# Three of eight w_out remainders on ScalarE and GpSimd in place of VectorE, and a new written order

## The chip, the cores and the metric

The kernel runs on one core of one Trainium2 chip. The core has five engines, each with a queue of its own that it works through in order: TensorE (PE in the profile; PEld is its loading of weights), VectorE (DVE), ScalarE (ACT), GpSimd (POOL) and SyncE (SP, which only issues transfers). Engines wait for one another through semaphores. The metric is the device time of one execution in microseconds (us).

## The reference

The reference is a Nystrom attention followed by a multiplicative feed-forward layer, with 8 batches, 8 heads, 576 positions, head size 64 and 32 landmarks:

```python
q_lm, k_lm = means of q and k over 18 neighbouring positions
A, Bm, C = softmax(q k_lm'), softmax(q_lm k_lm'), softmax(q_lm k')
Z = Bm' / (norms);  six times: Z = 2 Z - Z Bm Z
x = (A Z C v) as (4608, 512)
a, b = x @ w1, x @ w2
h = a * b @ w3
out = h @ w_out
```

All inputs and outputs are f32. The part that the change touches is small: the product of w3 (1024x1024) and w_out (1024x512). The kernel forms `w3 @ w_out` once, so that the last two lines become one product with a 1024x512 matrix, `w34`.

## The kernel before

**Two numbers for one.** TensorE works on f16 here. To keep the precision of w3 and w_out, the kernel splits each, scaled by `WSC` = 16, into a high part (the f16 nearest to it) and a remainder (the f16 nearest to what is left), and adds three products: high times high, high times remainder, remainder times high. For each of the eight slices c of w_out (128x512), ScalarE writes the high part (`woh{c}`, line 329) and VectorE the remainder (`wol{c}`, line 334), in one instruction that scales, subtracts and rounds:

```python
nc.vector.scalar_tensor_tensor(out=wo[:, 1, c, :], in0=wof[c // 2][:, c % 2, :], scalar=WSC,
                               in1=wo[:, 0, c, :], op0=ALU.mult, op1=ALU.subtract)
```

The f32 slices stand two by two in four buffers `wof`, which lie in space that later holds `u` and `ab`; the profile therefore names them `u` and `ab`.

**w3, a block row at a time.** For each of eight block rows j, four transfers bring 128x1024 of w3 (`w3n{j}`, three buffers), VectorE transposes it in two halves (`tr{j}0`, `tr{j}1`, line 340), ScalarE makes the high parts (`wh`, line 347) and VectorE the remainders (`wl`, line 355). TensorE then does eight steps `mm{j}0` to `mm{j}7` of three matmuls; for j = 0 they are split into `mh0{c}`-like first products (`mh{c}`, which need no remainder) and the other two (`mm0{c}`). `wo{j}` (line 388) stores the result.

**The attention, in sixteen quads** n (half a batch each). GpSimd's queue issues the K and Q loads (`lq{n}0`, `lq{n}1`, line 449) and the loads of w1 and w2 (`lw`, line 467). VectorE transposes (`T`, line 474). The landmark means come from TensorE for quads 0 and 1 (`mp`) and from GpSimd for all others (`ma`, `mb`, lines 482 and 489); ScalarE copies them (`mk`, lines 508 and 510) and VectorE turns them (`lt`). TensorE makes the scores (`S`, `A`). For `S`: VectorE's maximum `sm` (line 540), TensorE's `sw`, VectorE's `sb`, ScalarE's exponentials `se`, VectorE's `ct`. For `A`: VectorE's `ar` (line 583) and `am` (line 589), GpSimd's `as` (line 595), ScalarE's `ae`, VectorE's sums `au` (lines 609 and 610), GpSimd's `an` (line 623), VectorE's `aT` (line 632).

**The batches.** The batches stand in five groups of 1, 2, 2, 2 and 1. For each group TensorE and VectorE take turns in the iteration for Z (`N`, `no`, then `x{i}_0`, `y{i}_0` up to 4, `Z`, `zo`); then come `C`, `W` and `U` for each batch, the dense products `d` with `e` on ScalarE and `f` on VectorE, and the outputs `g`, `h` and `st`.

**The order.** Nothing orders itself at run time. `ORDER` (line 39) names all 1339 tasks one after another; each engine's queue is this list with the other engines' tasks left out. Numbers behind a colon choose buffers and PSUM banks. In the table of tasks, `deps` say who waits for whom.

**Gates.** Four small copies on GpSimd (`gw0` to `gw3`, line 394) each read one element of a w_out buffer, so that GpSimd's queue waits there until that buffer has landed. All K and Q loads from quad 2 on, and the loads of w1 and w2, stand behind the fourth. So w_out and the first of w3 do not share the transfer engines with them.

Of the kernel before, what the change touches and what calls it, by code (L numbers as in the profile page):

```python
# [11 lines left out]
ALU = mybir.AluOpType  # L12
# [27 lines left out]
w3n0a.0 w3n0.0:0 zz w3n0a w3n0 lq00:0 ca wu0:0 cc wf0a.0 wf0s.0 lq01 tab wf0s cb wf1s.0 lq10:1 wf1s lq11 wf2s.0  # L40
wf0a wf2s wf1a.0 wu1:1 wf1a wf2a.0 wu2:2 wf2a wu3:3 T00:0 cd tr00:4.0 wf3s.0 wh00 wl00 tr01:5 woh0 gw0 wf3s ce
mp0:6 woh1 wol0 wh01 mh0:7 wol1 mm00 mk0:0 wf3a.0 T01 mm01 wl01 lt0 T10:1 woh2 gw1 wf3a S0:0.1 A0:2.3 woh3 sm0:0
mh1 mh2 ar0:0 w3n1.0:1 mh3 sw0 mp1:4 wol2 w3n1.1 am0:1 w3n1.2 woh4 gw2 w3n1 wol3 w3n2.0:2 woh5 mh4 wol4 mm02
w3n2.1 mm03 wol5 w3n2.2 mh5 woh7 gw3 w3n2 mm04 T11 as0 mm05 w3n3.0:0 woh6 wol7 w3n3.1 mk1:1 mh6 lq20:2 wol6
w3n3.2 lq21 sb0 mm06 tr10:6.1 w3n3 se00:0 lq30:3 mh7 lt1 mm07 wh10 tr11:5 lq31 S1:2.3 ae0 wl10 lw00 w3n4.0:1
A1:4.0 wo0 w3n4.1 au0 lq40:0 mm10:6 wh11 w3n4.2 lq41 mm11 w3n4 ar1:1 bo0:0 an0:0 mm12 tr20:7.0 mm13 lq50:1 am1:2
wh20 se01 wl11 as1 tr21:0 mm14 wl20 lw10 wh21 w3n5.0:2 mm15 w3n5.1 aT0:0 ae1 ma2:0 mm20:4 wl21 w3n5.2 mm16 w3n5
sm1:3 mm17 au1 mm21 mb2 ct0:0 mm22 bo1 mm23 T20:0 mm24 tr30:1.1 sw1 T21 wh30 N0:5.4 mm25 tr31:7 an1:1 mk2:0 mm26
sb1 bt0 w3n6.0:0 wl30 w3n6.1 mm27 no0:0 lw11 wo1 w3n6.2 mm30:0 se10:1 lq51 wh31 lt2 mm31 ma3:0 T30:1 A2:1.6 wl31
x0_0:2 w3n6 tr40:5.0 mm32 y0_0:1 wh40 mm33 ar2:0 lq60:2 se11 mm34 mb3 wl40 wo2 S2:7.2 am2:5 mm40:1 T31 mm41  # L50
tr41:6 mm35 sm2:6 w3n7.0:1 x0_1:3 as2 mk3:1 lv0.0:0 aT1:1 mm36 y0_1:2 ct1:1 sw2 lq61 x0_2:5 wh41 lt3 ae2 T40:0
lq70:3 A3:4.3 w3n7.1 lq71 wl41 mm37 ma4:0 ar3:1 mm42 wo3 mm43 y0_2:0 am3:7 w3n7.2 mm44 sb2 tr50:6.1 se20:0 mm45
as3 au2 wh50 x0_3:3 mm46 w3n7 mb4 y0_3:1 ae3 tr51:4 mm47 wl50 wh51 au3 wo4 mm50:0 se21 mm51 lv0.1 bo2:1 T41
S3:5.7 an2:0 ct2:2 mk4:0 mm52 T50:1 x0_4:3 lq80:0 bo3 mm53 lt4 lv0.2 wl51 ma5:0 S4:6.1 aT2:2 mm54 sm4:8 A4:2.4
sm3:9 sw4 lv0 mm55 mb5 y0_4:2 sb4 T51 mm56 se40:1 tr60:3.0 mm57 se41 ar4:0 sw3 wh60 Z0:6 lv1.0:1 wo5 wl60 sb3
tr61:1 lq81 mm60:2 mk5:1 lv1.1 T60:0 an3:1 mm61 wh61 ct4:3 mm62 ma6:0 se30:0 lt5 mm63 lv1.2 wl61 se31 lv1 A5:4.0
T61 lv2.0:2 mm64 tr70:3.1 lv2.1 S5:5.1 am4:1 lw01 wh70 lv2.2 mm65 lq90:1 sm5:2 mm66 as4 wl70 mm67 lv2 aT3:3 sw5
mb6 tr71:7 mm70:3 ae4 lv3.0:3 sb5 ar5:1 mm71 lv3.1 se50:1 lv3.2 wh71 mm72 T70:1 lv3 C0:5.0 am5:4 wl71 as5 mk6:0
au4 lq91 se51 mm73 lv4.0:0 zo0:0 wo6 ma7:0 co0:0.5 lv4.1 ae5 ct3:0 lv4.2 W0:4 mm74 lt6 wp0:0 wq0 au5 S6:7.1 lv4
an4:0 U000:6.2.0.1 mm75 sm6:7 bo5 mb7 bo4 lv5.0:1 uo0001 A6:0.5 T71 uo0000 sw6 N1:4.0 sb6 T80:0 se60:0 lv5.1  # L60
U011:2.6 ar6:0 se61 uo0110 lv5.2 U001:7.1 bt1 am6:3 uo0111 an5:1 U010:0.5 lv5 uo0011 ct5:1 mm76 mk7:1 as6 T81
mm77 no1:0 C1:2.6 uo0010 ma8:0 ae6 uo0101 lt7 au6 wo7 uo0100 S7:1.7 lv6.0:2 co1:1.5 A7:4.5 mb8 lv6.1 sm7:1
d000:3.0 lv6.2 lv6 d010:2.6 ar7:1 e000:0 lv7.0:3 sw7 aT4:4 lv7.1 e010:1 x1_0:3 sb7 am7:4 lv7.2 se70:1 d002:4.5
lv7 y1_0:1 an6:0 se71 d011:2.1 f000:0 e002:2 d001:3.7 T90:1 e011:0 as7 mk8:0 d030:0.4 f002:1 f010 d022:2.5
lq100:2 f011 e030:2 x1_1:6 lq101 f030 e022:1 e001:0 C2:0.1 lt8 lq110:3 T91 bo6:0 ae7 ma9:0 y1_1:2 f001 f022
ct6:0 x1_2:2 lv8.0:0 A8:4.3 lv8.1 co2:0.0 lq111 lv8.2 d032:6.7 lq120:0 ar8:0 lv8 d020:5.0 mb9 e032:2 lv9.0:1
d031:1.3 f032 lv9.1 e020:0 y1_2:0 lv9.2 d012:4.6 f020 d021:7.5 am8:6 e012:1 g00:2 f012 e021:2 aT5:5 as8 mk9:1
au7 x1_3:0 S8:4.6 lq121 ae8 g01 lt9 f021 ma10:0 e031:0 y1_3:1 g30:7 h0:0 f031 sm8:9 g31 aT6:0 sw8 T100:0 h3:1
x1_4:5 mb10 S9:1.0 st3.0 sb8 T101 se80:0 A9:2.3 lv9 bo7 y1_4:2 g10:7 se81 st3 sm9:5 Z1:4 ct8:2 g11 zo1:1 an7:1
# [94 lines left out]
def kernel(  # L164
# [83 lines left out]
    def dve(cols):  # L248
        return 0.07 + cols / 960.0
# [142 lines left out]
    def gate(c):  # L392
        def fn():
            nc.gpsimd.tensor_copy(out=gates[:, c:c + 1], in_=wof[c][:, 1, 0:1])
        return fn
# [671 lines left out]
```

## Time and profile before

| | |
|---|---|
| median of 3 runs | 269.22 us (268.96 to 269.9) |
| the profiled execution | 268.93 us |
| its span, first to last instruction | 267.2 us |
| TensorE busy | 254.8 us |
| VectorE busy | 191.2 us |
| ScalarE busy | 161.5 us |
| GpSimd busy | 136.9 us |
| granted TensorE clock | 0.996 |
| transfers | 37.33 MB, mean 140 GB/s |

The last matmul ends at 262.4 us; the rest of the span is the last output's copy and its transfer. In rows of a view, "x8" is a count of instructions, "out<-in" names the tiles, and a bracket at the end of a timeline row gives the idle time of the engine before it and who ended it. A row of the chain gives start, length and what was at work. Neighbouring instructions on VectorE overlap by some 0.08 us in these rows, so that one of 0.68 us takes 0.60 us of its queue.

### The profile page before, as it was taken

How to read it: one execution, taken by the hardware profiler on the slowest of the kernel's cores; microseconds unless marked ns; L12 is line 12 of the kernel's file. 1: busy time of each engine (PE TensorE's matmuls, PEld its weight loads, DVE VectorE, ACT ScalarE, POOL GpSimd, SP SyncE). 2: the span in 40 equal slices, each digit the busy share in tenths (PEclk: the TensorE clock that was granted, in tenths of full speed). 3: DMA queues.
4: the chain of work that ended last, by engine and by line, in shares of the span. 5: the costliest groups of instructions: out<-in, count | busy, mean ns of one | idle time of the engine just before them, and what ended most of it. 6: DMA issues, size and time to landing. Idle time of an engine off the chain costs nothing.

```text
span 267.2 us, 9564 instructions
## 1 busy us (share of the span) xinstructions
PE 254.8 (95%) x3948; PEld 167.4 (63%) x3948; DVE 191.2 (72%) x458; ACT 161.5 (60%) x415; POOL 136.9 (51%) x159
## 2 busy tenths in 40 slices
PE   8688999999999999999999999999999999999992
PEld 3343444344568955689868457877866699467662
DVE  1799999999999999999999787643672267203340
ACT  2555364745597467988757899634115975564452
POOL 4548999999999999999787511000110000000000
PEclk9999999999999999999999999999999999999998
DMA  7999999999966896289903333232713020415355
GB/s 173 277 233 213 234 238 231 240 261 234 200 156 178 146 245 140 51 179 250 160 9 82 81 83 81 66 81 60 206 55 83 4 61 2 92 28 139 80 119 139
DMA packets 22668, 37.33 MB, mean 140 GB/s; under 512 B 3552, under 2 KB 7904, under 8 KB 22624
## 3 DMA queue, kind: packets, MB, share of 16 engines
q1 hardware_dynamic: 16240, 24.33, 36.4%
q0 software_dynamic: 5696, 11.54, 24.3%
q10 hardware_dynamic: 688, 0.85, 1.0%
q8 instruction: 31, 0.51, 0.9%
q14 instruction: 13, 0.11, 0.1%
HBM read 38.80 MB, written 9.44 MB: 181 GB/s over the span
## 4 chain that ended last, share of the span: by engine, by line
PE 67%; POOL 14%; DVE 7%; ACT 5%; issue 3%; DMA 2%; DVEq 0%; POOLq 0%; ACTq 0%
PE bank L245 67%; POOL ls L489 5%; POOL ls L482 4%; DMA nat<-in_k_dram 2%; ACT lm L510 2%; POOL ea L595 2%; DVE bank L340 1%; DVE wo L334 1%; POOL nat L449 1%; ACT u L833 1%; DVE tiny L609 1%; DVE T L474 1%; POOL w L467 1%; ACT ec L559 1%; DVE tiny L589 1%
## 5 line engine op out<-in xcount | busy, mean ns | idle before, releaser
L914 DVE TENSOR_TENSOR ab<-asb,bank 128x384 f16<-128x384 f16 x96 | 49.4, 543 | 36.6 <-ACT asb L908 33.7
L245 PE MATMUL bank<-aT,u 128*128 128x192 f16 x768 | 69.4, 246 | 0.0
L245 PE MATMUL bank<-w,ab 128*128 128x512 f16 (+1 forms) x296 | 69.1, 374 | 0.0
L245 PEld LDWEIGHTS <-u 128*128 128x128 f16 x768 | 63.6, 98 | 6.0 <-issue 0.6
L908 ACT CAST asb<-bank 128x384 f16<-128x384 f32 x96 | 43.9, 487 | 27.4 <-PE bank L245 21.6
L245 PE MATMUL bank<-wo,w3t 128*128 128x512 f16 x192 | 46.3, 380 | 2.7 <-DVE wo L334 2.1
L245 PEld LDWEIGHTS <-ab 128*128 128x128 f16 x296 | 27.5, 98 | 26.3 <-issue 2.2
L489 POOL TENSOR_TENSOR ls<-ls 128x128 f32<-128x128 f32 (+2 forms) x56 | 40.8, 729 | 3.8
L928 ACT ACTIVATE osb<-bank 128x512 f32<-128x512 f32 x35 | 21.0, 605 | 28.3 <-PE bank L245 26.3
L623 POOL TENSOR_TENSOR ah<-ea,tiny 128x576 f16<-128x576 f32 x16 | 18.6, 1162 | 35.2 <-DVE tiny L711 26.7
L833 ACT CAST u<-bank 128x512 f16<-128x512 f32 x64 | 34.0, 616 | 3.0 <-PE bank L245 3.0
L482 POOL TENSOR_TENSOR ls<-nat 128x1152 f32<-128x1152 f16 x14 | 33.4, 2384 | 1.3 <-ACT asb L908 0.7
L245 PEld LDWEIGHTS <-w3t 128*128 128x128 f16 x192 | 17.3, 98 | 24.5 <-issue 5.1
L474 DVE STREAM_TRANSPOSE T<-nat 128x576 f32<-128x576 f32 x32 | 24.0, 750 | 5.6 <-DMA nat<-in_k_dram 5.6
L595 POOL TENSOR_TENSOR ea<-ea,tiny 128x608 f32<-128x608 f32 x16 | 19.8, 1241 | 9.6 <-DVE tiny L589 6.0
L559 ACT ACTIVATE ec<-bank,tiny 128x288 f32<-128x288 f32 x32 | 16.0, 502 | 7.1 <-DVE tiny L551 7.0
L245 PE MATMUL bank<-T 32*32 32x288 f16 (+1 forms) x320 | 18.5, 291 | 1.6 <-DVE T L516 1.6
L245 PE MATMUL bank<-vb,ecT 64*64 64x128 f32 x576 | 18.7, 272 | 0.0
L245 PEld LDWEIGHTS bank<-vb,ecT 64*64 64x64 f32 x576 | 16.7, 133 | 1.9 <-ACT u L833 0.4
L347 ACT ACTIVATE w3t<-bank 128x512 f16<-128x512 f32 x16 | 9.5, 593 | 12.3 <-DVE bank L340 12.1
L245 PE MATMUL bank<-w,wT 64*32 64x512 f16 x512 | 16.8, 378 | 0.0
L245 PE MATMUL bank<-xz 32*32 32x64 f32 (+1 forms) x768 | 16.5, 214 | 0.2 <-DVE xz L768 0.2
(78 smaller groups left out, 299.9 us busy)
## 6 DMA issues: line engine op xcount, KB each, us to landing
vb<-in_v_dram SPq DMA_DIRECT2D x64, 144.0 KB, 4.6
out_dram<-osb SPq DMA_DIRECT2D x70, 128.0 KB, 2.8
nat<-in_k_dram POOLq DMA_DIRECT2D x16, 288.0 KB, 8.6
nat<-in_q_dram POOLq DMA_DIRECT2D x16, 288.0 KB, 7.4
w3n<-in_moe_w_dram SPq DMA_DIRECT2D x30, 128.0 KB, 8.3
w<-in_moe_w_dram POOLq DMA_DIRECT2D x4, 512.0 KB, 12.4
ab<-in_moe_w_out_dram SPq DMA_DIRECT2D x8, 128.0 KB, 6.0
u<-in_moe_w_out_dram SPq DMA_DIRECT2D x4, 128.0 KB, 6.5
```

Source lines behind the costliest of these rows:

```text
L245: nc.tensor.matmul(out_, lhsT, rhs, start=start, stop=stop, **({} if pos is None else {"tile_position": pos}))
L347: nc.scalar.activation(out=w3t[at(f"w3t{j}")][:, 0, 4 * h:4 * h + 4].rearrange("p e g i -> p (e g i)"), in_=bank(at(f"w3f{j}{h}")), func=A ...
L474: nc.vector.transpose(out=Ts[at(f"T{n}")][:, GRP * t:GRP * t + GRP] .rearrange("p r l e -> p (r l e)").bitcast(FP32), in_=nats[at(f"nat{n} ...
L482: nc.gpsimd.tensor_tensor(out=l, in0=nat[:, :, 0:9, :], in1=nat[:, :, 9:18, :], op=ALU.add)
L489: nc.gpsimd.tensor_tensor(out=l[:, :, x:x + m, :], in0=l[:, :, x:x + m, :], in1=l[:, :, y:y + m, :], op=ALU.add)
L559: nc.scalar.activation(out=ecs[at(f"ec{n}")][:, hp, :], in_=two(f"pS{n}")[hp][:, 0:288], func=AXF.Exp, scale=SCALE, bias=t[:, 2 + hp:3 + h ...
L595: nc.gpsimd.tensor_tensor(out=ea, in0=ea, in1=tinies[at(f"ta{n}")][:, 0:19].unsqueeze(2).to_broadcast([128, 19, M]), op=ALU.subtract)
L623: nc.gpsimd.tensor_tensor(out=ahs[at(f"ah{n}")].rearrange("p g m r -> p g r m"), in0=eas[at(f"ea{n}")][:, 0:GRP, :].rearrange("p (g r) m - ...
L833: nc.scalar.copy(out=uu[at(f"u{b}{qd}")][:, wi, 512 * half:512 * half + 512], in_=bank(at(f"pU{b}{wi}{half}{qd}")))
L908: nc.scalar.copy(out=asb[at(f"as{b}{j}{ch}")], in_=d1_ps(b, j, ch)[0])
L914: nc.vector.tensor_mul(abts[at(f"ab{i // 2}")][:, 2 * j:2 * j + 2, CH * (i % 2):CH * (i % 2) + CH], asb[at(f"as{b}{j}{ch}")], d1_ps(b, j, ...
L928: nc.scalar.activation(out=osb[at(f"os{i}")], in_=bank(at(f"pE{i}")), func=AXF.Copy, scale=2.0 ** -12)
```

## The change

For the slices 3, 5 and 7 the remainder is made in two steps. ScalarE first scales the f32 slice in place (`wos{c}`, after `woh{c}`), then GpSimd subtracts the high part (`wol{c}`). The other five remainders stay on VectorE. The gates read the even slice of each buffer, which is not overwritten.

```diff
+    def wout_scale(c):
+        def fn():
+            x = wof[c // 2][:, c % 2, :]
+            nc.scalar.activation(out=x, in_=x, func=AXF.Copy, scale=WSC)
+        return fn
+
+    def wout_pool(c):
+        def fn():
+            nc.gpsimd.tensor_tensor(out=wo[:, 1, c, :], in0=wof[c // 2][:, c % 2, :], in1=wo[:, 0, c, :],
+                                    op=ALU.subtract)
+        return fn
...
     def gate(c):
         def fn():
-            nc.gpsimd.tensor_copy(out=gates[:, c:c + 1], in_=wof[c][:, 1, 0:1])
+            nc.gpsimd.tensor_copy(out=gates[:, c:c + 1], in_=wof[c][:, 0, 0:1])
...
+                    if c in (3, 5, 7,):
+                        add(f"wos{c}", "ACT", 0.52, wout_scale(c), deps=[f"woh{c}"], at=("o", 1.0 + 0.1 * c), kind="wo")
+                        add(f"wol{c}", "POOL", 1.11, wout_pool(c), deps=[f"wos{c}", f"woh{c}"],
+                            at=("o", 1.0 + 0.1 * c), kind="wo")
+                        continue
                     add(f"wol{c}", "DVE", dve(512), wout_lo(c), deps=[f"wf{c // 2}s", f"wf{c // 2}a", f"woh{c}"],
```

`ORDER` is replaced as a whole. Every other task is the same; its place, its buffers and its banks may differ. The beginnings of the queues, with the buffer numbers left out, and two later stretches:

```text
TensorE before: wu0 wu1 wu2 wu3 mp0 mh0 mm00 mm01 S0 A0 mh1 mh2 mh3 sw0 mp1 mh4 mm02 mm03 mh5 mm04 mm05 mh6 mm06 mh7 mm07
  S1 A1 mm10 mm11 mm12 mm13 mm14 mm15 mm20 mm16 mm17 mm21 mm22 mm23 mm24 sw1 N0 mm25 mm26
TensorE after:  wu0 wu1 wu2 wu3 mp0 mh0 mm00 mm01 S0 A0 mh1 mh2 mh3 mp1 mm02 sw0 mh4 mm03 mh5 mh6 mm04 mm05 mm06 mh7 mm07
  A1 mm10 mm11 S1 mm12 mm13 mm14 mm15 mm16 mm17 mm20 sw1 mm21 mm22 N0 mm23 mm24 mm25 mm26

VectorE before: zz ca cc T00 cd tr00 wl00 tr01 wol0 wol1 T01 wl01 lt0 T10 sm0 ar0 wol2 am0 wol3 wol4 wol5 T11 wol7 wol6 sb0
  tr10 lt1 tr11 wl10 au0 ar1 tr20 am1 wl11 tr21 wl20 aT0 wl21 sm1 au1 ct0 T20 tr30 T21 tr31
VectorE after:  zz ca cc tr00 tr01 wl00 T00 wl01 cd T01 wol0 wol1 lt0 sm0 ar0 T10 wol2 am0 T11 wol4 sb0 wol6
  tr10 tr11 lt1 wl10 au0 tr20 ar1 wl11 am1 wl20 ct0 tr21 T20 sm1 au1 tr30 T21 wl21 wl30
  later, before: lt7 au6 co1 sm7 ar7 aT4 sb7      after: aT4 no1 lt7 T81 au6 co1 sm7 ar7

ScalarE before: w3n0a wf0a tab wf0a wf1a wf1a wh00 woh0 woh1 wh01 mk0 woh2 woh3 woh4 woh5 woh7 woh6 mk1 se00 wh10 ae0
ScalarE after:  w3n0a wf0a tab wf0a wf1a wh00 wh01 wf1a woh0 woh1 mk0 woh2 woh3 wos3 woh5 woh4 wos5 woh6 woh7 wos7 mk1 wh10 ae0

GpSimd before:  lq00 lq01 cb lq10 lq11 gw0 ce gw1 gw2 gw3 as0 lq20 lq21 lq30 lq31 lw00 lq40 lq41 an0 lq50 as1 lw10 ma2 mb2
GpSimd after:   lq00 lq01 lq10 cb ce lq11 gw0 wol3 gw1 gw2 as0 wol5 gw3 lq20 lq21 wol7 lq30 lq31 lq40 lw00 lq41 lq50 an0 lw01 as1 ma2 lq51 mb2
  later, before: mb7 an5 as6 ma8                   after: mb7 as6 lq100 ma8 an5
```

`w3n0a`, `wf0a` and `wf1a` are transfers that ScalarE's queue issues (w3's first block row, and parts of w_out). SyncE's queue holds its loads of w_out and w3 in the same order in both.

More of the change, by code (lines that the diff above doesn't have):

```diff
@@ L39 @@
 ORDER = """
[L40 to L69, printed above, removed]
@@ L117 @@
+e721:0 st28 e732:1 f721 d722:6.4 st30.0 f731 d712:3.0 e722:0 f732 st30 h31:1 g330:2 f722 e712:2 st31.0 g331 f712
+st31 g340:5 st32 h33:3 g341 st33.0 st33 g350:6 h34:0 st34.0 g351:7 h350:1 st34 h351 st3501 st3511 st3500 st3510
 """
```

121 lines of the change are left out of this document (74 added, 47 removed).

## The prediction

> **What bounds the kernel now.** I read the page first, then the chain of work that ended last, then busy time by stage, with the borders of the stages taken from the chain.
>
> ```profile
> span 267.2 us, 9564 instructions
> PE 254.8 (95%) x3948; PEld 167.4 (63%) x3948; DVE 191.2 (72%) x458; ACT 161.5 (60%) x415; POOL 136.9 (51%) x159
> PE 67%; POOL 14%; DVE 7%; ACT 5%; issue 3%; DMA 2%; DVEq 0%; POOLq 0%; ACTq 0%
> ```
>
> The whole span says "TensorE, 95%". That is an average over stages. The chain in order of time (start, length, what) shows three:
>
> ```profile
> 20.63 0.68 DVE wo L334
> 21.41 0.73 DVE bank L340
> 25.93 0.66 DVE tiny L589
> 26.67 1.20 POOL ea L595
> 28.49 2.39 POOL ls L482
> 68.95 1.05 ACT lm L510 x4
> 81.94 0.82 DVE tiny L540 x2
> 82.81 2.22 PE bank L245 x48
> ```
>
> VectorE carries the chain up to 26.6 us, GpSimd from 26.67 to about 68.8, ScalarE and VectorE up to 82.8, and TensorE from there on. The first line is one of the remainders that the change touches, so the work that is moved does stand on the chain. The piece at 82.81 belongs to `x1_0`, the first iteration of the second group; I call it the hand-over. The stages (us, then busy us of PE, PEld, DVE, ACT, POOL, clock, DMA share, GB/s):
>
> ```profile
> 9.40:21.41 12.01, 8.15 (x78) 4.54 (x79) 11.58 (x22) 7.20 (x20) 8.15 (x20) 1.00 1.10 243
> 21.41:81.94 60.53, 58.96 (x742) 30.02 (x742) 58.59 (x136) 36.40 (x103) 57.79 (x62) 1.00 1.03 219
> 82.81:262.43 179.62, 179.40 (x3098) 129.46 (x3098) 117.58 (x283) 115.17 (x289) 67.28 (x70) 1.00 0.45 103
> ```
>
> After the hand-over TensorE is busy for 179.40 of 179.62 us. Counted in the two orders, the TensorE tasks ahead of `x1_0` are the same set, and so are those behind it. So the change can pay, or cost, only in when `x1_0` starts; the 179.6 us behind it I leave as they are. Between 21.41 and 81.94 VectorE is idle for 60.53 - 58.59 = 1.9 us: it is the engine to watch there, with GpSimd next (2.7 us idle).
>
> **The change part by part.** *Three remainders leave VectorE.* The rows around them:
>
> ```profile
> 17.21 0.68 DVE L334 SCALAR_TENSOR_TENSOR wo<-u,wo 128x512 f16<-128x512 f32 x1
> 17.81 1.28 DVE L334 SCALAR_TENSOR_TENSOR wo<-ab,wo 128x512 f16<-128x512 f32 x2
> 19.02 0.77 DVE L474 STREAM_TRANSPOSE T<-nat 128x576 f32<-128x576 f32 x1
> 21.41 0.73 DVE L340 STREAM_TRANSPOSE bank<-w3n 128x512 f32<-128x512 f32 x1
> w3n<-in_moe_w_dram SPq DMA_DIRECT2D x1, 128.0 KB, 5.5
> ```
>
> From 17.21 to 17.81, and twice from 17.81 to 19.02, one takes 0.60 us of the queue; three are 1.8 us. All three stand ahead of `tr10`, the transpose at 21.41. If VectorE's own queue were all that held `tr10`, it would start at 19.6. But `tr10` reads the second tile of w3. Its fourth piece was issued between 15.7 and 16.0 us, and the last row says 5.5 us to landing: 21.2 to 21.5. The queue of transfers is full there (share 1.10, 243 GB/s), and the change takes no byte away from what lands ahead of it. So data and engine arrive together in the kernel before, and I take the gain at `tr10` as 0, not 1.8 us; both ends are kept. What is late next is the transfer.
>
> *ScalarE scales in place.* The nearest row is the high part, of the same shape and engine:
>
> ```profile
> 15.83 1.15 ACT L329 ACTIVATE wo<-ab 128x512 f16<-128x512 f32 x2 [2.11 <-DMA ab<-in_moe_w_out_dram]
> 18.08 1.15 ACT L329 ACTIVATE wo<-ab 128x512 f16<-128x512 f32 x2 [1.10 <-DMA ab<-in_moe_w_out_dram]
> ```
>
> That is 0.57 us each, 1.7 us for three, next to 3.2 us in which ScalarE waited for w_out. Queued behind the last is `mk1`, which then ends at about 20.7 and not 20.2; `lt1`, which needs it, stands behind `tr10` anyway. Cost 0; if `mk1` slipped beyond 22.5 each further us would count in full.
>
> *GpSimd subtracts.* No row has this operation. The nearest: 128x512 of f32 at 1.28 us, and 128x608 at 1.21 (minimum, median, maximum in the second row).
>
> ```profile
> L489 POOL TENSOR_TENSOR ls<-ls 128x512 f32<-128x512 f32 x14 | 17.9, 1279 | 0.5
> L595 POOL TENSOR_TENSOR ea<-ea,tiny x16: 1200/1210/1666, 18.5 to 161.1; 128x608 f32<-128x608 f32 x16
> L334 DVE SCALAR_TENSOR_TENSOR wo<-ab,wo x4: 678/679/999, 17.8 to 20.6; 128x512 f16<-128x512 f32 x4
> 16.52 0.77 DVE L589 TENSOR_REDUCE tiny<-ea 128x19 f32<-128x608 f32 x1
> 18.12 0.41 POOL L394 COPY gates<-ab 128x1 f32<-128x1 f32 x1 [2.07 <-DMA ab<-in_moe_w_out_dram]
> 18.50 1.67 POOL L595 TENSOR_TENSOR ea<-ea,tiny 128x608 f32<-128x608 f32 x1
> 20.11 0.63 POOL L449 DMA_DIRECT2D nat<-in_k_dram  x1
> 24.75 1.16 POOL L623 TENSOR_TENSOR ah<-ea,tiny 128x576 f16<-128x576 f32 x1 [0.71 <-DVE tiny L610]
> POOL gates L394 <- DMA ab<-in_moe_w_out_dram: 3.2, 2, 2.1
> ```
>
> I take 1.2 us each (1.0 to 1.3 if the cost goes with the columns), 3.6 in all. The idle time that can hide it is 3.2 us at the gates and 0.71 at the row of 24.75. Now the queue, with what waits behind each step. `wol3` stands ahead of the second gate and waits for ScalarE; behind it wait gates, `as0` and all later K and Q loads. `as0` now stands ahead of the last gate: after `am0`, which ended at 17.29 (16.52 and 0.77 long), it runs to 18.5, `wol5` to 19.7, the gate to 19.9. So the load at 20.11 goes out 0.2 us earlier. Two loads (1.15), `wol7` (1.2), six loads of about 0.6, `an0` (1.16), a load of w1/w2 moved up here (0.65) and `as1` (1.2) follow: 19.9 + 1.15 + 1.2 + 3.5 + 1.15 + 0.65 + 1.2 = 28.75. There `ma2` starts, which stood at 28.49 on the chain: +0.26. The other route to it is `am1` (chain, 25.93): it is moved behind one w3 remainder of 0.6, which gives `as1` at 27.3 and `ma2` at 28.5, inside that. From `ma2` up to the end of `mb7` GpSimd's two lists hold the same work. I carry +0.3.
>
> One of the sixteen `as` rows is long, 1.67 against 1.21: `as0`, which began while VectorE was in a remainder (18.41 to 19.09, by the rows at 17.81), and the longest remainder, 0.999 against 0.679, ran while `as0` did. So each such meeting costs 0.3 to 0.5 us on one side. Three remainders and `as0` beside VectorE's own could meet up to four times: 0 to 1.9 us on GpSimd.
>
> By the Trainium skill (SBUF — State Buffer, "Who interferes with whom") a VectorE instruction with two SBUF inputs and a GpSimd instruction that reads SBUF exclude each other on a shared port, and the second waits until the first is done. The trace agrees, with 1666 against 1210 ns. By that rule alone a meeting costs at most the rest of the other instruction, an estimate of up to 0.68 us, and the sum below would be up to 2.7 us higher.
>
> *Loads moved in front.* The second q load stands behind the constants `ce`; these hold the queue for 5 us in the kernel before, from the first row here to the second, and now stand right behind the first loads, from about 3.4; so the load goes out at some 8.3, 5 us later.
>
> ```profile
> 9.55 1.05 POOL L292 TENSOR_SCALAR swapneg<-ident 128x32 f32<-128x32 f32 x4
> 14.53 0.18 POOL L394 COPY gates<-u 128x1 f32<-128x1 f32 x1
> nat<-in_q_dram POOLq DMA_DIRECT2D x1, 288.0 KB, 11.5
> ```
>
> The third row is that load: 11.5 us, behind three others. With the same latency it lands at 19.8, and `T11`, which needs it, would push `tr10` by 0.4; behind the same three it lands near 14.9 as now. I take 0. One w_out piece stands behind the first two w3 high parts on ScalarE, some 2 us later than before; `wos3`, and so `wol3`, slip by up to 2 us, of which the gates' idle time covers all but about 0.6. That is the upper end for `ma2` without meetings: +0.9.
>
> *VectorE's order from `tr10` to `sm7` (81.94).* Compared as sets, the new list holds one task more, `aT4`: +0.4 us (its rows last 0.45). And one wait goes:
>
> ```profile
> 77.01 1.16 POOL L623 TENSOR_TENSOR ah<-ea,tiny 128x576 f16<-128x576 f32 x1
> 78.12 1.21 POOL L595 TENSOR_TENSOR ea<-ea,tiny 128x608 f32<-128x608 f32 x1
> 80.11 0.79 DVE L609 TENSOR_REDUCE tiny<-ea 128x19 f32<-128x608 f32 x1 [0.55 <-ACT ea L603]
> ```
>
> `as6` (78.12) stood behind `an5` (77.01); now it stands ahead of it, 1.1 us sooner, so the 0.55 us wait of `au6` goes. What is late next is `lt7`, which waits for `mb7` by way of ScalarE.
>
> *TensorE's order.* `mm24` now stands behind `sw1` and `N0`, and its w3 remainder behind six VectorE tasks:
>
> ```profile
> 28.68 0.65 DVE L355 SCALAR_TENSOR_TENSOR w3t<-bank,w3t 128x512 f16<-128x512 f32 x1
> 33.60 0.68 DVE L340 STREAM_TRANSPOSE bank<-w3n 128x512 f32<-128x512 f32 x1
> 32.64 0.28 PE L245 MATMUL bank<-tiny,swapneg 128*128 128x2 f32 x2
> ```
>
> The six took 29.3 to 33.6, so that remainder, with `aT0` (0.4) gone from ahead of it, ends near 33.3 rather than 29.3. `mm24` ran just ahead of the third row, which is `sw1`; with `sw1` and `N0` in front of it TensorE is there at about 32.5 and stands still for 0.8 us. What hides it: VectorE is not delayed by it, and the hand-over waits for VectorE. If TensorE itself set the hand-over, the 0.8 would count.
>
> **The sum** at the hand-over: `tr10` 0, GpSimd +0.3 of which VectorE's slack takes half (+0.15), `aT4` +0.4, `au6` -0.55: 0.0. The profiled execution took 268.93 us (span 267.2 and 1.7 around it), and so stands 0.3 below the median of 269.22. The forecast is no change: 269.2.
>
> **The rivals.** *A, faster: the transfer does not hold `tr10`.* Against it stands the landing at 21.2 to 21.5; for it, that VectorE reached `tr10` without a gap, so the trace does not show a wait for the data, and that the loads ahead of it are reordered. If w3's tile lands sooner, up to 1.8 us come through; if half does, with the same sum otherwise, 268.3; all of it 267.4. Fewer meetings with GpSimd in the crowded stretch work the same way.
>
> *B, slower: GpSimd gets late.* The chain runs on GpSimd from 26.67 to 68.8, and the three subtractions are put ahead of that. Place: `ma2`. Its price is its slip beyond what VectorE's later waits forgive. I let them forgive 0.5 us (the one wait that goes), so it decides from 29.8 on (28.49 + 0.5 + 0.8): `lt4`, `lt7` and `au5` then each wait. With two meetings (+0.9) on top of the late `wol3` (+0.9) it starts at 30.3, and the time is 269.2 + 1.3 = 270.5; with four, 271.5.
>
> *C: TensorE's new order sets the hand-over.* Then the 0.8 us at `mm24` counts: 270.0. Against it: VectorE had 1.9 us idle in 60.5.
>
> **How the numbers follow.** A measurement of this kernel tells about 0.3% (0.8 us) from no change. No change, 268.4 to 270.0: 0.36, with half of C. A beyond 0.8 us: 0.31, since several small terms point that way. B and the rest of C: 0.33, since most of what is new stands in the queue that carries the chain. The range leaves out the far tails of A and B: 267.2 to 271.3.
>
> **What would show it.** In the profile after: `tr10` starting at 21.2 to 21.5 with idle time before it says the transfer holds it; a start below 20.5 is A. GpSimd's subtraction at 1.0 to 1.3 us, `ma2` at 28.5 to 29.4; later is B. `au6` without a wait, `sm7` near 81.9, `x1_0` near 82.8, then 179.6 us to the last matmul. I am wrong if the part behind `x1_0` changes by over 0.5 us, for I priced its new order at nothing.

## The result and the profile after

The changed kernel is slower, by about 1%. Its median was 273.38 us against 269.56 for the kernel before in the same session: a ratio of 1.0105 (95% interval 1.0064 to 1.0145). Three later measurements, unaltered, gave 1.011 (1.0055 to 1.0165), 1.0073 (1.0012 to 1.0134) and 1.0095 (1.0058 to 1.0132). The forecast, no change at 269.2 us within 267.2 to 271.3, was wrong.

The profiled execution took 274.24 us. Its page:

```profile
span 272.5 us, 9579 instructions
PE 256.5 (94%) x3948; PEld 167.8 (62%) x3948; DVE 192.4 (71%) x455; ACT 163.1 (60%) x418; POOL 140.3 (51%) x162
PE 74%; POOL 8%; DMA 7%; DVE 4%; ACT 4%; issue 2%; ACTq 0%; SPq 0%; DVEq 0%; POOLq 0%
```

Busy times hardly moved; VectorE is not less busy (192.4 against 191.2), though three instructions left it. The chain of work that ended last, by this view, went from VectorE to the transfers of w_out and GpSimd. Some of its pieces in order of time (start, length, what; the lines are those of the changed file):

```profile
14.13 5.41 DMA ab<-in_moe_w_out_dram
19.64 1.16 ACT wo L328 x2
20.82 0.64 ACT ab L334
21.52 0.76 POOL wo L339
23.07 0.57 POOL gates L405
24.79 1.18 POOL wo L339
30.99 1.23 POOL ea L611
32.22 2.31 POOL ls L498
```

This answers the first chain of the prediction. There VectorE's remainder (20.63) and `tr10` (21.41) led. Here the view puts the last of w_out, two high parts and a scaling ahead of GpSimd's subtraction, but that link is no real wait: the scaling at 20.82 is `wos7`, and the subtraction at 21.52 is `wol5`, which needs `wos5` (ended at 19.46). `wol5` starts when `as0`, ahead of it in GpSimd's queue, ends (timeline):

```profile
20.35 1.21 POOL L611 TENSOR_TENSOR ea<-ea,tiny 128x608 f32<-128x608 f32 x1 [0.61 <-DVE tiny L605]
```

So what GpSimd waited for was VectorE's `am0`, when all of w_out had landed (19.54); in f1 and k1, the same kernel again, the chain has `as0` in that place. From `as0` on GpSimd's queue leads, through `wol5`, the last gate, `wol7` (24.79) and `as1` (30.99) to `ma2`, at 32.16 instead of 28.49.

This profile overstates the change in two ways. First, the landmark means `mp0`, TensorE's first work on the inputs, wait for the second K/Q load. The timelines of the kernel before and of the changed one:

```profile
10.21 0.77 PE L245 MATMUL bank<-nat,ident 128*128 128x128 f16 x11 [1.56 <-DMA nat<-in_q_dram]
```

```profile
12.14 0.83 PE L244 MATMUL bank<-nat,ident 128*128 128x128 f16 x12 [3.05 <-DMA nat<-in_q_dram]
```

In the twenty executions profiled here `mp0` starts from 9.98 to 12.34, in old and new order alike. Second, the granted clock is low here between 12 and 18 us (stretches of 3 us; the last three figures are clock, DMA share and GB/s):

```profile
12.00:15.00 3.00, 2.86 (x23) 1.59 (x23) 2.30 (x4) 1.04 (x5) 0.00 (x0) 0.70 1.08 278
15.00:18.00 3.00, 3.00 (x35) 1.39 (x34) 1.91 (x5) 1.99 (x4) 0.14 (x1) 0.73 0.97 213
```

In the trace this is one stretch of 3.41 us at 0.50. Nine of the twenty have such a dip between 9 and 18 us, old and new order alike (h3 has one at 23.1, f1 a second at 25.0); the first profile of the kernel before has none. So I took further profiles, among them k2 of the changed kernel at full clock and k3 of the kernel before with a dip, and compare like with like. The table counts `ma2` and `x1_0` from `mp0` (`x1_0` itself starts at 83.12 in the kernel before; the piece at 82.81 that the prediction calls `x1_0` opens with `sw7`, just ahead of it); "rest" is from `x1_0` to the end of the last matmul. The ratio is from many runs. "Equal clock" is the difference to the kernel before in us by one least-squares fit to 304 runs, with a level for each kernel and one common slope for the run's mean clock (it comes to 1.58 us for 0.01); its 95% intervals are about 0.5 either way, 0.4 for the changed kernel. Seven slow runs, each over 1.5% above the fastest of its kernel, are left out of it.

| kernel | clock 9 to 18 | mp0 | ma2 | x1_0 | rest | ratio (95%) | equal clock |
|---|---|---|---|---|---|---|---|
| before | full | 10.21 | 18.28 | 72.91 | 179.31 | 1 | 0 |
| k3 before, again | low | 11.49 | 18.72 | 73.46 | 179.32 | 0.9977 (0.9948 to 1.0006) | 0 |
| changed | low | 12.14 | 20.02 | 74.15 | 180.80 | 1.0105 (1.0064 to 1.0145) | +2.2 |
| f1 changed, again | low | 11.21 | 19.76 | 74.50 | 180.24 | 1.011 (1.0055 to 1.0165) | |
| k1 changed, again | low | 11.34 | 19.56 | 73.61 | 180.53 | 1.0073 (1.0012 to 1.0134) | |
| k2 changed, again | full | 11.11 | 18.96 | 73.09 | 180.81 | 1.0095 (1.0058 to 1.0132) | |
| e1 new order, all VectorE | full | 10.20 | 18.16 | 73.09 | 179.60 | 1.0023 (0.9988 to 1.0059) | +0.9 |
| h1 e1, piece early | full | 10.33 | 18.55 | 73.61 | 181.34 | 1.0036 (1.001 to 1.0061) | +1.4 |
| f3 e1, rear altered | full | 10.37 | 18.40 | 72.77 | 181.47 | 1.0082 (1.0045 to 1.0119) | +2.3 |
| e2 piece early | full | 11.19 | 18.60 | 72.75 | 180.33 | 1.0042 (1.0002 to 1.0082) | +1.5 |
| e5 fills | full | 11.20 | 18.71 | 72.80 | 180.30 | 1.0064 (1.0021 to 1.0107) | +2.0 |
| h3 early and fills | full | 10.65 | 18.71 | 73.38 | 180.50 | 1.0089 (1.0054 to 1.0124) | +2.0 |
| e4 GpSimd front of before | full | 9.98 | 19.33 | 73.41 | 180.44 | 1.0047 (1.0005 to 1.0089) | +1.5 |
| f2 rear of before | low | 10.85 | 20.22 | 75.09 | 180.14 | 1.0081 (1.0045 to 1.0116) | +1.8 |
| f4 early, rear of before | low | 12.34 | 19.28 | 73.41 | 180.84 | 1.0079 (1.0042 to 1.0116) | +1.6 |
| e3 engines, old order | full | 12.04 | 19.36 | 73.97 | 179.31 | 1.0031 (0.999 to 1.0071) | +1.0 |
| h2 e3, fills | low | 10.88 | 20.13 | 74.77 | 179.59 | 1.0029 (1.0006 to 1.0052) | +1.0 |
| e6 before, piece late | full | 10.76 | 18.48 | 73.19 | 179.54 | 1.0001 (0.9963 to 1.0038) | +0.8 |
| e7 before, new rear | low | 11.39 | 18.06 | 72.83 | 181.32 | 1.0036 (1.0007 to 1.0065) | +2.4 |
| e8 before, as6 first | low | 11.53 | 18.92 | 73.23 | 179.77 | 1.0000 (0.9961 to 1.004) | -0.1 |

By these single profiles the change brings `x1_0` 0.18 us later at full clock (k2 against before), with the dip 0.15 to 1.04 (against k3). Behind it, it loses 0.93 to 1.50 us in all four profiles, at either clock. (`tr10` waits for a transfer that does not move with `mp0`, so a late start is partly caught up, and counting from `mp0` favours k2, which started 0.9 later. On the plain clock `x1_0` is 1.08 later in k2 than in the first profile, and at the same 84.95 in k1 and k3.)

The stages, in k2 (the borders are `tr10`, `sm7`, `x1_0` and the last matmul), and the last one in the kernel before:

```profile
9.40:21.50 12.10, 8.37 (x77) 4.50 (x78) 10.14 (x18) 8.36 (x21) 5.29 (x7) 1.00 1.07 241
21.50:83.02 61.52, 58.28 (x739) 29.05 (x738) 59.42 (x139) 36.21 (x103) 59.77 (x66) 1.00 1.05 218
84.20:265.00 180.80, 180.42 (x3097) 130.20 (x3096) 117.56 (x282) 114.70 (x288) 67.42 (x69) 1.00 0.44 101
```

```profile
83.12:262.43 179.31, 179.09 (x3097) 129.16 (x3096) 117.27 (x283) 115.06 (x288) 67.05 (x69) 1.00 0.45 103
```

In the last stage TensorE shows 1.3 us more busy time for the same 3097 matmuls at the same clock.

### The profile page after: what moved, and what is told of

Same layout as the page of the kernel before. It is cut to its first block, busy times and chain, and to the rows that moved or that the text cites. A ratio compares the mean times of both kernels' runs of the same rounds, so it can differ in the third digit from the quotient of the medians.

```text
span 272.5 us, 9579 instructions
## 1 busy us (share of the span) xinstructions
PE 256.5 (94%) x3948; PEld 167.8 (62%) x3948; DVE 192.4 (71%) x455; ACT 163.1 (60%) x418; POOL 140.3 (51%) x162
## 4 chain that ended last, share of the span: by engine, by line
PE 74%; POOL 8%; DMA 7%; DVE 4%; ACT 4%; issue 2%; ACTq 0%; SPq 0%; DVEq 0%; POOLq 0%
PE bank L244 74%; DMA ab<-in_moe_w_out_dram 5%; POOL ls L505 2%; POOL nat L465 2%; POOL ls L498 2%; DMA w3n<-in_moe_w_dram 1%; ACT lm L526 1%; ACT u L849 1%; POOL wo L339 1%; POOL ah L639 1%; DVE tiny L556 1%; DVE bank L351 0%; DVE T L490 0%; DVE w3t L366 0%; POOL ea L611 0%
## 5 line engine op out<-in xcount | busy, mean ns | idle before, releaser
L244 PE MATMUL bank<-wo,w3t 128*128 128x512 f16 x192 | 47.4, 386 | 4.2 <-POOL wo L339 1.9
L244 PE MATMUL bank<-w,wT 64*32 64x512 f16 x512 | 17.3, 379 | 0.0
L244 PEld LDWEIGHTS bank<-xz 32*32 32x32 f32 x768 | 12.8, 104 | 6.4 <-issue 4.2
```

Of the source, the lines that this page charges most:

```text
L244: nc.tensor.matmul(out_, lhsT, rhs, start=start, stop=stop, **({} if pos is None else {"tile_position": pos}))
```

## The experiments

**e1: the new order with all eight remainders on VectorE.**

```diff
-                    if c in (3, 5, 7,):
+                    if c in ():
  ORDER: wos3, wos5, wos7 taken out; wol7 moved up to stand behind wol6
```

> The new order, but with all eight remainders on VectorE again (no scaling in place; the three stand where the GpSimd ones stood in the written order, the last right behind the one of slice 6). Three theories. L (lock): VectorE's remainders and GpSimd's instructions shut each other out of SBUF, which cost VectorE's 2.0 us ahead of tr10 and GpSimd 1.3 us; then the remainders are 0.68 us again apart from one that meets as0, the last K/Q gate comes some 1.5 us sooner, ma2 near 30, and the time is 271 to 271.5. P (late piece): the last piece of w_out's second buffer, which stands behind two w3 high parts on ScalarE's queue, landed at 15.9 instead of 12.1 and holds everything behind it; then ma2 stays near 31 and the time near 272.5. O (the order as a whole is worse, wherever the remainders are made): 273 or more.

Measured: 1.0023, +0.9 at equal clock. The order alone costs something under half. Behind `x1_0` it took 179.60 us, only 0.29 more than the kernel before.

**e2: the changed kernel, the second half of w_out's piece 1 issued ahead of `wh00`, as before.**

```diff
- wf2a wu3:4 tr01:5 wh00 wl00 wh01 wf3s.0 wf1a
+ wf2a wu3:4 tr01:5 wf1a wh00 wl00 wh01 wf3s.0
```

> The changed kernel with one word of the order moved: the piece of w_out that ScalarE's queue issues last stands ahead of the two w3 high parts again, as in the kernel before. P: it lands near 12.5 and not 15.9, the first scaled slice is ready near 14, GpSimd's first subtraction starts near 14.5 and not 17.9, ma2 comes 1.5 to 2.5 us earlier (30), and the time falls by 1.5 to 2 us to about 271.5. L: the piece is early but the meetings stay, so that ma2 moves by under 1 us and the time stays above 272.5. O: no change, 273.4.

Measured: 1.0042, +1.5. ScalarE's queue in the changed kernel (timeline):

```profile
5.97 1.19 ACT L358 ACTIVATE w3t<-bank 128x512 f16<-128x512 f32 x2 [2.32 <-DVE bank L351]
9.12 0.32 ACTq L312 DMA_DIRECT2D u<-in_moe_w_out_dram  x1
```

The high parts end at 7.2; the issue goes out at 9.12, because it uses the same completion semaphore as an earlier piece, which landed at 9.10. In e2 it went out by 4.9. The meetings stay (GpSimd's `wol5` 1.60, VectorE's `wol6` 1.58 us).

**e3: the engines alone, in the old order.**

```diff
- sm0:0 mh1 ... woh5 mh4 wol4 ... mh5 woh7 gw3
+ wos3 sm0:0 mh1 ... woh5 wos5 mh4 wol4 ... mh5 woh7 wos7 gw3
```

> The change of engines alone: the order of the kernel before, with the three scalings put right behind their high parts and the three remainders on GpSimd at the places in the list where VectorE made them. L: GpSimd's three subtractions, at 16 to 22 us, meet VectorE's five, each meeting 0.4 to 0.9 us; tr10 near 21.5 to 22.5, ma2 1 to 2.5 us later than 28.5, the time 270 to 271.5. P: the piece is issued early as before, so the engines alone cost nothing: 269.2 within 0.5. O: the same, 269.2, or a little faster since VectorE has 1.8 us less to do.

Measured: 1.0031, +1.0; behind `x1_0` exactly the 179.31 us of the kernel before. Here all of the loss lies ahead of `x1_0`. With `wol3` and `wol5` in front of it, `as0` starts 9.07 us behind `mp0` and not 8.29, and from there to `ma2` GpSimd is idle for 0.16 us, against 0.95 in the kernel before.

**e4: the changed kernel with `cb`, `lq11` and `gw0` in GpSimd's old places.**

```diff
- lq10:1 ... cb ce ... lq11 ... gw0
+ cb lq10:1 ... lq11 ... gw0 ce
```

> The changed kernel with GpSimd's front as before: all four K and Q loads of quads 0 and 1 ahead of the constants, the constants behind the first gate. In the changed kernel the first K and Q tiles landed at 9.5 and 12.0 instead of 7.6 and 10.1, although they were issued at the same time. D: GpSimd's constants, which ran from 3.5 to 7.7 us there, hold up the transfers that its own queue has issued; then these tiles land at 7.6 and 10.1 again, the first TensorE means start at 10.2 and not 12.1, and the time falls by 0.5 to 1.5 us. P and L: the front has slack against what they hold, so the landings may move but ma2 and the time stay (272.5 to 273.5).

Measured: 1.0047, +1.5, with the meetings as before (VectorE's `wol2` 1.34, `wol4` 1.22, `wol6` 1.57). The constants ahead of that load, priced at 0, may cost up to 1 us; the intervals leave it open.

**e5: the changed kernel with zero fills in place of GpSimd's subtractions.** GpSimd stays busy, but reads nothing.

```diff
-            nc.gpsimd.tensor_tensor(out=wo[:, 1, c, :], in0=wof[c // 2][:, c % 2, :], in1=wo[:, 0, c, :],
-                                    op=ALU.subtract)
+            for _ in range(3):
+                nc.gpsimd.memset(wo[:, 1, c, :], 0.0)
```

> The changed kernel with each of GpSimd's three subtractions replaced by three fills of the same tile with zero, which write SBUF and read nothing (so three slices lose their remainder; all else, the order and the scalings on ScalarE too, is kept). L (lock: VectorE's remainder reads two SBUF operands and shuts out a GpSimd instruction that reads SBUF, and the other way round): VectorE's remainders of slices 2 and 6 go back from 1.25 and 1.6 us to 0.68, the one of slice 4, which meets a GpSimd subtraction of the attention, stays near 1.2; tr10 starts within 0.2 us of the landing of the second w3 tile and not 1.4 us after it. The time falls below the changed kernel's by 1 to 2 us. Without the lock (GpSimd and VectorE only share bandwidth, or the long remainders come from the transfers): the remainders stay long beside any GpSimd work.

Measured: 1.0064. VectorE's timeline (two remainders and `tr10`), of the changed kernel and of e5:

```profile
20.89 1.23 DVE L345 SCALAR_TENSOR_TENSOR wo<-ab,wo 128x512 f16<-128x512 f32 x1
22.10 1.57 DVE L345 SCALAR_TENSOR_TENSOR wo<-ab,wo 128x512 f16<-128x512 f32 x1
23.59 1.30 DVE L351 STREAM_TRANSPOSE bank<-w3n 128x512 f32<-128x512 f32 x2
```

```profile
18.52 1.23 DVE L345 SCALAR_TENSOR_TENSOR wo<-ab,wo 128x512 f16<-128x512 f32 x1
19.75 0.68 DVE L345 SCALAR_TENSOR_TENSOR wo<-ab,wo 128x512 f16<-128x512 f32 x1
21.47 1.32 DVE L351 STREAM_TRANSPOSE bank<-w3n 128x512 f32<-128x512 f32 x2 [1.04 <-DMA w3n<-in_moe_w_dram]
```

The 1.57 us became 0.68 with fills running beside it throughout: a remainder is held up by GpSimd's reading, not by its writing. (The 1.23 runs beside `as0` in both.) And the freed VectorE then stands still for 1.04 us until w3's tile lands. At equal clock e5 gains nothing clear (+2.0 against +2.2).

**e6: the kernel before with the piece late.**

```diff
- wu1:1 wf1a wf2a.0 ... wf3s.0 wh00 wl00
+ wu1:1 wf2a.0 ... wf3s.0 wh00 wf1a wl00
```

> The kernel before with one word of its order moved: the last piece of w_out that ScalarE's queue issues stands behind the first w3 high part. It is then issued near 9.2 us instead of 4.7. P (the late piece alone costs): it lands near 14 to 15 instead of 12.1, the high part of slice 2 starts 2 us later, VectorE's third remainder at 16.5 instead of 15.9, the second K/Q gate waits, and the time rises by 0.5 to 1 us. Other theory: in this order nothing but two high parts waits for it, the last gate (18.1) and ma2 (28.5) stay where they are, and the time stays within 0.3 us; then a late piece costs only where GpSimd's queue waits for what is made from it.

Measured: 1.0001 against its own session, +0.8 in the fit over all sessions. The trace has `x1_0` 0.28 later, counted from `mp0`. Somewhere between; open.

**e7: the old order up to `x1_0`, the new one behind it, all on VectorE. e8: the kernel before with `as6` ahead of `an5`.**

```diff
  e7 ORDER: the words up to x1_0 of the old list, then the rest of the new list (buffers given anew where taken)
  e8 ORDER:
- an5:1 U010:0.5 lv5 uo0011 ct5:1 mm76 mk7:1 as6
+ as6 an5:1 U010:0.5 lv5 uo0011 ct5:1 mm76 mk7:1
```

> All on VectorE as in the kernel before, the old order up to the first iteration of the second group (x1_0), and behind it the new order (20 buffers renumbered where they were still in use). R (the new order is worse behind that point: it puts 1.1 us more of VectorE's work ahead of sm11, which still sets TensorE's pace there): x1_0 stays at 83.1 in a run with the same start, from x1_0 to sw11 the kernel takes 40.6 and not 39.8 us, and the time rises by 0.4 to 1.2 us. My prediction's step (the part behind x1_0 is TensorE's alone and the same set of work): no change, within 0.3 us.

> The kernel before with two neighbours on GpSimd's queue exchanged: as6 ahead of an5. If the 0.55 us wait of VectorE's au6 for it reaches the first iteration of the second group, as the prediction had it, x1_0 starts 0.3 to 0.55 us sooner and the time falls by about as much (0.1 to 0.2%). If VectorE waits elsewhere instead (aT5, or the maximum sm7 behind TensorE), au6 starts sooner but x1_0 does not, and the time is the same within 0.1%.

Measured: e7 1.0036, with 72.83 us ahead of `x1_0` and 181.32 behind it: a new rear alone can make the loss. But e7 loses elsewhere than the changed kernel does. Right behind `x1_0`, at the seam of the two lists, TensorE stands idle for 0.77 us (for ScalarE's exponentials) and 0.51 (for its copies), and in all it is busy for 179.59 of 181.32 us, where k2 has 180.42 of 180.80. e8 1.0000: the wait of `au6` is gone, and nothing comes of it.

**f1 to f4: the changed kernel again; with the rear of before; e1 with two of VectorE's pieces later; piece early and rear of before.**

```diff
  f2, f4 ORDER: the words up to x1_0 of the new list, then the rest of the old list (buffers given anew where taken)
  f4 as well:
- tr01:5 wh00 wl00 wh01 wf3s.0 wf1a
+ tr01:5 wf1a wh00 wl00 wh01 wf3s.0
  f3 ORDER (on top of e1): ct10 and f201 moved from ahead of sm11 to right behind it
```

> The changed kernel once more, unaltered, beside its variants. Before, its ratio was 1.0105 (1.0064 to 1.0145), and its profiled execution had TensorE's first product 1.93 us later than the profiled execution of the kernel before, which I put down to the landing of the second K/Q load (12.00 us against 10.07). In other executions that landing lay anywhere from 9.85 to 12.00 us, whatever the kernel. If that is right, a new profile may have it earlier, and the span is then 272.5 less the difference; the ratio without it is about 2.7 us, 1.010, and should stand again between 1.006 and 1.012. If a landing at 12.0 belongs to the change, it is at 12.0 again. Behind the hand-over (x1_0) the last TensorE instruction should end 180.3 to 180.8 us later (179.3 in the kernel before): that does not depend on the start.

> The changed kernel's engines and order up to x1_0, and from there the order of the kernel before. Theory O (the new order costs up to 1.5 us behind the hand-over): from the start of x1_0 to the end of the last TensorE instruction 179.2 to 179.5 us as in the kernel before (180.8 in the changed one), no stall of 0.3 us or more between C3 and A10, U111 and d200, x3_3 and g151; the time 0.8 to 1.5 us under the changed kernel's, ratio 1.004 to 1.007. Rival L (all of the loss arises ahead of the hand-over, the rear only inherits it): 180.3 us or more again, and the changed kernel's ratio.

> All eight remainders on VectorE in the new order, and two pieces of VectorE's work (ct10 and f201) moved from ahead of sm11 to behind it. If the stall ahead of sw11 comes from these two (1.1 us of VectorE ahead of the softmax), d220 to sw11 loses less than 0.1 us and x1_0 to the last instruction takes about 179.3 us (179.6 without the move). If they are not the cause, 179.6 stays or grows, and the stalls C3 to A10 (0.39) and U111 to d200 (0.45) stand in either case. The time is within 0.4 us of the same kernel without the move, ratio 0.999 to 1.004.

> As the run with the new front and the old rear, with the second half of w_out's piece 1 issued ahead of ScalarE's wh00 again. Only the meetings of VectorE's and GpSimd's remainders are left of what I count as losses. If the three causes add up (late piece, meetings, rear), wf1a lands near 13, an0 starts by 27, ma2 by 29.8 with an ordinary start, x1_0 to the last instruction takes 179.3 us, and the ratio is 1.001 to 1.004. If the engines alone cost more than that, it stays at 1.005 or above. If ScalarE's and GpSimd's help is worth something once the rest is undone, it is below 0.999.

Measured: f1 1.011, f2 1.0081, f3 1.0082, f4 1.0079. f2 and f4 did not come out as theory O had it: behind the new front the old rear took 180.14 and 180.84 us. Task by task TensorE lost 0.67 and 1.00 us near the seam, from the start of `C2` to that of `x1_2`: 2.96 and 3.28 us, against 2.34 in the kernel before and 2.49 to 2.63 in the changed one. The stall lies inside `C2` (0.55 and 0.87 us), where its second bank is emptied by a ScalarE copy; ScalarE had just waited 1.35 and 1.67 us for a landmark mean of GpSimd. So part of GpSimd's lateness passes into the rear.

In the kernel before, the chain behind 82.81 is nothing but TensorE for over 50 us. In f1 it leaves TensorE for VectorE, ahead of `sw11`: `f201` and `f202`, then the softmax's maximum `sm11`.

```profile
125.15 1.01 DVE ab L930 x2
126.45 0.45 DVE tiny L556
126.95 15.18 PE bank L244 x241
```

f3 moved `ct10` and `f201` behind `sm11`. Its chain:

```profile
122.68 0.77 DVE tiny L556 x2
124.09 0.53 DVE ab L930
124.66 3.38 PE bank L244 x63
```

Now TensorE's `d220` needs the bank that `f201` (124.09) empties, and loses 1.45 us. VectorE owes TensorE both at that place. (In e1's own profile TensorE lost nothing ahead of `sw11`, so f3 had little to gain.)

**h1, h2, h3: how the parts divide.** h1 is e1 with the piece early, h2 is e3 with fills, h3 is e2 with fills.

```diff
  h1 (on top of e1), h3 (on top of the changed kernel):
- tr01:5 wh00 wl00 wh01 wf3s.0 wf1a
+ tr01:5 wf1a wh00 wl00 wh01 wf3s.0
  h2 (on top of e3), h3:
-            nc.gpsimd.tensor_tensor(out=wo[:, 1, c, :], ..., op=ALU.subtract)
+            for _ in range(3):
+                nc.gpsimd.memset(wo[:, 1, c, :], 0.0)
```

> New order, all eight remainders on VectorE, and the second half of w_out's piece 1 issued ahead of ScalarE's wh00: the order alone. The same kernel with the late piece had its fastest run at 270.0 us where the fastest of the kernel before had 269.0, and the late piece put into the old order made the fastest run 0.6 us longer (269.4 against 268.8). If the late piece is what the order costs ahead of x1_0, this run is 0.3 to 0.6 us faster than with it: fastest run near 269.5, ratio 0.999 to 1.002, wf1a landing by 13.5, x1_0 to the last TensorE instruction 179.3 to 179.7. If the order's cost lies elsewhere (rear), the fastest run stays at 270.0 or more.

> The old order with ScalarE's three scalings, and zero fills in place of GpSimd's three subtractions: three 512-column slices of w_out lose their remainder, so the output differs. With the subtractions in the same order the fastest run was 269.8 us (before 269.0), and VectorE's remainders met them at 1.10 to 1.57 us instead of 0.68. Theory L (the meetings are the cost of the engines): no remainder over 0.7 us except one beside as0, ratio 0.998 to 1.001, fastest run within 0.3 us of the kernel before. Rival (GpSimd's or ScalarE's own time is the cost, not the reading): the ratio stays at 1.003 and the fastest run 0.8 us above.

> The changed kernel with the piece early and zero fills in place of GpSimd's three subtractions (three 512-column slices of w_out lose their remainder, so the output differs). The two repairs alone brought the ratio from 1.0105 to 1.0042 (piece) and 1.0064 (reading). If they add up, little is left ahead of x1_0: ma2 starts by 29.0 with an ordinary start, x1_0 to the last instruction takes 179.5 to 180.3 us, ratio 1.000 to 1.004, the rest being the order's rear. If they are two names of one loss (the same stretch of waiting seen twice), the ratio stays at 1.004 to 1.006.

Measured: h1 1.0036, h2 1.0029, h3 1.0089. h1 and h2 came out as the rival in their expectations had it, and h3 worse than either reading. With all remainders on VectorE the early piece gains nothing (+0.9 without it, +1.4 with), taking away the reading gains nothing in the old order (+1.0 and +1.0), and with both repairs the changed kernel is about as slow as without. A fill is no neutral stand-in, though: three take 1.7 us, a subtraction 1.17. What is left is GpSimd's time (h2, h3) and the rear (h1, h3).

**k1, k2, k3: the clock.** The two kernels unaltered.

> The changed kernel, unaltered, for one more profile. In all eight kernels that have the new order and GpSimd's three pieces, ma2 starts 11.8 to 11.9 us behind as0, GpSimd being without idle time between them; as0 starts 6.8 to 7.5 us behind mp0 where the granted clock was 1.00 between 9 and 18 us, and 7.5 to 8.4 where it was not. If the low clock is what makes the front late, a profile at full clock has as0 at 6.8 to 7.5, ma2 at 18.6 to 19.3 and x1_0 at 72.7 to 73.5 behind mp0. If the late piece and the meetings do it at any clock, as0 is at 7.9 or more, ma2 at 19.7 or more and x1_0 at 74.0 or more. With a low clock: as0 7.9 to 8.4 again, which tells nothing new. From x1_0 to the last matmul 180.2 to 180.8 in each case.

> The same kernel once more, in case the other profile falls on a low clock: full clock as0 6.8 to 7.5, ma2 18.6 to 19.3, x1_0 72.7 to 73.5 behind mp0 if the clock is the cause; as0 7.9, ma2 19.7, x1_0 74.0 or more if it is not. From x1_0 to the last matmul 180.2 to 180.8.

> The kernel before, unaltered, for a second profile. Its first had clock 1.00 throughout and x1_0 72.91 behind mp0; two kernels with its front had the low clock and 72.83 and 73.23. In its order the last gate stands ahead of as0, so the K and Q loads do not wait for the landmark path. If that makes it forgive the low clock, a profile with one has x1_0 at 72.8 to 73.3; if the low clock costs the old front as much as the new one, 73.8 or more. At full clock 72.9 again. From x1_0 to the last matmul 179.3 to 179.6.

Measured: k2 has full clock, and the front that its expectation gave for that (`as0` 7.14, `ma2` 18.96, `x1_0` 73.09 behind `mp0`). k1 and k3 have the dip: `as0` at 7.77 in k1, `x1_0` at 73.61, and 73.46 in the kernel before. Against the profiles at full clock that is 0.55 us for the old front and 0.5 to 1.4 for the new one; but e7 and e8, with the old front and the dip, have `x1_0` at 72.83 and 73.23, so what the dip costs the old front may be nothing. In k2 GpSimd runs from `as0` to `ma2` without idle time (timeline, without the load issues and `an0`):

```profile
18.25 1.21 POOL L611 TENSOR_TENSOR ea<-ea,tiny 128x608 f32<-128x608 f32 x1 [0.61 <-DVE tiny L605]
19.43 1.60 POOL L339 TENSOR_TENSOR wo<-ab,wo 128x512 f16<-128x512 f32 x1
20.97 0.65 POOL L405 COPY gates<-ab 128x1 f32<-128x1 f32 x1
22.69 1.18 POOL L339 TENSOR_TENSOR wo<-ab,wo 128x512 f16<-128x512 f32 x1
28.89 1.23 POOL L611 TENSOR_TENSOR ea<-ea,tiny 128x608 f32<-128x608 f32 x1
30.07 2.37 POOL L498 TENSOR_TENSOR ls<-nat 128x1152 f32<-128x1152 f16 x1
```

That is 11.82 us; in all ten profiles with the new order and GpSimd's three pieces it is 11.79 to 11.91. In e1 the same stretch takes 10.76, with 1.7 us idle in it. So in the changed kernel every delay of `as0`, by the clock or by a meeting, reaches `ma2` undiminished.

Pieces of k2's chain also show how the rear lost its slack another way, by a K/Q load that GpSimd issues late and a landmark mean behind it:

```profile
119.03 0.54 POOL nat L465
119.56 7.47 DMA nat<-in_q_dram
127.19 2.38 POOL ls L498
137.69 0.89 DVE ea L599 x2
138.62 1.59 PE bank L244 x48
```

No version beat the kernel before; e8 equals it.

## Why the prediction was wrong

**The step that failed: "the 179.6 us behind it I leave as they are".** I took 179.40 us busy of 179.62 as proof that TensorE's order there could not matter. But in these traces a busy matmul can be a waiting one: 180.42 of 180.80 is as busy, and 1.5 us longer. From `x1_0` on, the old rear behind the old front took 179.31 to 179.77 us in six profiles, the new one 179.60 to 181.47 in twelve; the changed kernel's four lie at 180.24 to 180.81, 1.28 us above before on the mean. Comparing starts task by task against the shortest such step, TensorE loses 0.38 us between `C3` and `A10`, 0.45 between `U111` and `d200` and 0.3 ahead of `sw11` in each of the four; the kernel before loses less than 0.25 at every one of these steps. The first two stand in e1 as well, which took only 179.60, so they explain little of the 1.28. What the four have beyond e1 is the 0.3 ahead of `sw11`, 2.49 to 2.63 us from `C2` to `x1_2` (2.19 in e1), and in two of them 0.35 and 0.62 between `x3_3` and `g151`. What holds TensorE is shown for `sw11` alone; the rest of the cause stays open. I had named a move of over 0.5 us there as what would prove me wrong, but gave it no chance and no place in the range.

**The front came near the forecast in one profile, not over all runs.** Forecast: `ma2` +0.3, `x1_0` 0.0. Measured in k2, from `mp0`: +0.68 and +0.18 (on the plain clock +1.58 and +1.08). The queue that I counted, from `as0` at 17.3 to `ma2` at 28.75, was 11.45 us; it is 11.82. That 0.5 us of a slip at `ma2` is forgiven fits k2 (0.68 less 0.5 is 0.18), but one pair of profiles does not show it. Over all runs, 2.2 us less the 1.28 behind `x1_0` leave some 0.9 ahead of it, about what the engines cost in the old order (e3, h2).

**Rival B, GpSimd late, is most likely the rest.** Its point, `ma2` at 29.8, is 19.6 behind `mp0`; two of the four profiles of the changed kernel are past it (20.02, 19.76), one stands on it (19.56), k2 is not. It has to have a slow front first, and it is the smaller part. Of its two terms, the late piece was issued 4.4 us later in the profiled execution and 3.2 in k2, not 2: the landing of an earlier transfer held it, not only the two high parts. The meetings, "0 to 1.9 us on GpSimd" taken as 0, all came in the first profile: `wol5` 1.60 for 1.17, two gates 0.64 for 0.18, 1.36 us in all, and on VectorE 2.0 us (1.25, 1.23, 1.57 for 0.68 each), as much as the three remainders that left it saved (1.8).

**How the runs divide it.** At equal clock the engines in the old order cost 1.0 us (e3, h2), the order with all on VectorE 0.9 and 1.4 (e1, h1); together 1.8 to 2.3, and the changed kernel stands at +2.2. Which term of the front makes GpSimd's share is not settled: the early piece alone stands at +1.5, the fills alone at +2.0, both together at +2.0, and that differs by little more than the intervals.

**A price on the low side.** A meeting was put at 0.3 to 0.5 us; it costs up to 0.9 (1.57 less 0.68). By the Trainium skill (SBUF — State Buffer, "Who interferes with whom") the second instruction waits for the rest of the first, and the estimate from that, 0.68 us, was nearer. The trace agrees with the rule: 0.68 us beside fills, which read nothing, 1.57 beside a subtraction.

**What held.** The subtraction at 1.2 us (1.16 to 1.18 where nothing met it). `tr10` at 0: where VectorE came early, as in e5, it waited for w3's tile, so rival A falls, and the 1.8 us freed has no use there. `au6`'s wait is gone. Rival C falls: `mm24` loses no more than before. ScalarE's scalings at 0 held: the one that the chain shows ahead of a subtraction (20.82) is not what that subtraction waited for.

**The base.** 269.22 was the median of three runs. Over 137 later runs of the kernel before it is 270.6, from 268.8 to 273.0, so the forecast's time stood on the low side, and only ratios and differences are used here.

## What to carry to other kernels

Work taken off a busy engine pays only if what that engine waits for next comes sooner; look for the transfer behind it first, and do not put the work into the queue that carries the chain, where it takes away the idle time that used to absorb a slow start. A written order is priced along its whole length: a stage with TensorE 99.9% busy can still grow by 1.5 us, so compare starts of the same tasks, not busy shares. And before two profiles are compared, see that they started alike and ran at the same clock; one profile of each can mislead by more than the effect.

## What the runs showed that I had not expected

The start of `mp0` varies by 2.4 us from execution to execution with the landing of the first K/Q loads. The granted clock falls to 0.50 for 3.41 us near the start in ten of the twenty executions profiled, in old and new order alike. An issue can wait for the landing of an earlier transfer with the same completion semaphore (7.2 to 9.12 us on ScalarE's queue). And a one-element copy on GpSimd took 0.64 instead of 0.18 us beside a VectorE remainder.
